# The last weight matrix of a decode kernel: five loads in place of eight, and all its rows summed in one way

## The chip, the cores and the metric

The kernel runs on one core of a Trainium2 chip. TensorE does the matmuls (PE in the profile; PEld is its weight load), VectorE (DVE), ScalarE (ACT) and GpSimd (POOL) the rest, and SyncE (SP) issues nearly all loads. The metric is the device time of one execution in microseconds (us), less is better. Before the change it is 401.04 us, the median of four runs: 400.88, 401.01, 401.08 and 402.25.

## The reference

Two blocks read the same normalised row of 1024 numbers, and their results are added. Block A is attention for one new token over a cache of 65536 keys, with 32 query heads in 4 groups. Block B is a small MLP. All inputs are bfloat16.

```python
q = (x @ wq).reshape(B, Sq, 32, 128)                    # A: x is 1 x 1024
scores = einsum("bhqd,bhkd->bhqk", q, k) * 128 ** -0.5  # k, v: 4 groups, 65536 keys each
o = einsum("bhqk,bhkd->bhqd", softmax(scores), v) @ wo

h  = gelu(layernorm(x) @ w1)                            # B
x1 = x + shifted(h) @ w2                                # S is 1
h2 = gelu(layernorm(x1) @ w3) @ w4                      # w4: 3584 x 1024
return x + A + x1 + h2
```

With one token the shifts of the MLP's mixer leave zeros, so the kernel multiplies w2 by a column of zeros. The change touches only the last product of block B, `h @ w4`, and the store of the result.

## The kernel before, in words

**Loads.** Every large input goes once through SBUF in three buffers of 64 KB a partition (`big`, SLOTS = 3). The class `Stream` holds the order: wq, w3, w1 and w2 together, then K and V of each of eight units, with wo between the last K and the last V, and w4 at the end. `pump` issues the next load on SP's queue (line 172 to 191) when a buffer is free; `done` frees one. A key unit is 32768 keys, 8 MB of K or V. w4 is 7 MB and is issued in the pieces of `W4_PIECES`: 6, 5, 6, 4, 3, 2, 1 and 1 rows (lines 181 to 186). A "row" of w4 here is 1024 numbers on each of 128 partitions, 2 KB a partition; there are FC = 28 of them. Each piece has a semaphore of its own, so TensorE can start on a piece as soon as that piece has landed.

**A key unit.** `compute_k` transposes K on VectorE in four parts (line 359), multiplies by the queries (line 364), takes the maximum and the exponentials (lines 369 to 382) and transposes the probabilities (line 385). `compute_v` multiplies them by V (line 414).

**The result row.** `psB` is one PSUM bank; the first half of the result row stands in partitions 0 to 31 and the second half in partitions 32 to 63, each repeated 32 times, since the left operand is a column broadcast to 32. `row_acc` (line 222) adds one product of 512 columns to one half. Everything that adds to the result goes through it: the input row, the w2 products, the projected rows of groups 0 to 2 (`add_projection`, line 457), the projection of group 3 (`project(3)`, 16 matmuls with `oT`, line 451) and w4 (`compute_w4`, two matmuls of 512 columns a row, line 467). The two halves sit in different column groups of TensorE's array.

**The tail.** The order in which the lines are written is: K of the last unit; the projections of groups 0 to 2 with wo; `add_projection`; V of the last unit with `group_rows` (lines 430 to 444, which end in `oT` of group 3); w4's rows 0 to 10; `project(3)`; w4's rows 11 to 21; and then the part that the change removes. A scheduler of the framework may move an instruction past others on its engine when its inputs are late by its own estimate.

**The last six rows.** Rows 22 to 27 are summed in another way. `quarter_acc` splits the result row into four quarters of 256 columns, in two PSUM banks and four column groups, so that a row costs four matmuls of 256 columns. Rows 22 to 24 (AHEAD = 3) come first. Meanwhile ScalarE copies the sums so far out of `psB` (line 486, `sums`), TensorE adds them to the quarters by fp32 matmuls with single columns of the identity (line 504), and rows 25 to 27 follow. ScalarE copies one half of the quarters to `out_t` (line 509), VectorE the other (line 510), and ScalarE issues the store (line 511). For this the quarters of a half lie 256 columns apart in `out_t`, and the two rows that are stored are partitions 31 and 32.

Of the kernel before, what the change touches and what calls it, by code (L numbers as in the profile page):

```python
# [8 lines left out]
BF16 = mybir.dt.bfloat16  # L9
F32 = mybir.dt.float32  # L10
# [5 lines left out]
P = 128  # L16
# [1 line left out]
SUBS = 4  # L18
SETS = 4
SLOTS = 3  # L20
W4_PIECES = (6, 5, 6, 4, 3, 2, 1, 1)
NARROW = 6
AHEAD = 3


def keep_loaded_weights(nc):
# [68 lines left out]
def kernel(  # L95
# [14 lines left out]
    nc = tc.nc  # L110
# [3 lines left out]
    D = A_x.shape[-1]  # L114
# [7 lines left out]
    FC = F // P  # L122
    UKEYS = P * ROW // DH
    assert DH == P and HQ // HKV == 8 and HKV == 4 and D == 1024 and F == 3584 and S == 1
    assert SK % UKEYS == 0 and sum(W4_PIECES) == FC
    NB = SK // UKEYS
# [8 lines left out]
    ogpool = ctx.enter_context(tc.tile_pool(name="og", bufs=2))  # L135
    ps_S = ctx.enter_context(tc.tile_pool(name="psS", bufs=1, space=bass.MemoryType.PSUM))
    ps_O = ctx.enter_context(tc.tile_pool(name="psO", bufs=1, space=bass.MemoryType.PSUM))
    ps_M = ctx.enter_context(tc.tile_pool(name="psM", bufs=2, space=bass.MemoryType.PSUM))
# [10 lines left out]
    class Stream:  # L149
# [17 lines left out]
        def load(self, it):  # L167
# [13 lines left out]
            elif it == "w4":  # L181
                w4_v = B_w4.rearrange("(m c) n -> m c n", c=FC)
                c0 = 0
                for n in W4_PIECES:
                    go(out=t[:, c0 * D:(c0 + n) * D], in_=w4_v[:, c0:c0 + n, :].rearrange("p c n -> p (c n)"))
# [7 lines left out]
    st = Stream()  # L193
# [6 lines left out]
    ident_f = const.tile([P, P], F32, name="ident_f")  # L200
# [9 lines left out]
    for b in range(2):  # L210
        nc.gpsimd.tensor_copy(
            out=spread[:, 2 * b:2 * b + 2, :].rearrange("p r (a i) -> p r a i", a=4),
            in_=ident_f[:, 64 * b:64 * b + 64].rearrange("p (i r) -> p r i", r=2).unsqueeze(2).to_broadcast([P, 2, 4, 32]))
# [6 lines left out]
    psB = ps_B.tile([P, 512], F32, name="psB")  # L220

    def row_acc(j, lhsT, rhs, start=False):
        nc.tensor.matmul(psB[32 * j:32 * j + 32, :], lhsT=lhsT.to_broadcast([lhsT.shape[0], 32]), rhs=rhs, start=start,  # L223
                         stop=False, tile_position=(0, 32 * j), skip_group_check=True)

    x_t = ppool.tile([P, DC, 32], BF16, name="x_t", tag="p")
    for a in range(4):
        nc.vector.transpose(out=x_t[32 * a:32 * a + 32].rearrange("p c j -> p (c j)"),  # L228
                            in_=x_row[:, 256 * a:256 * (a + 1)].rearrange("p (i c) -> p c i", c=DC))
# [3 lines left out]
    def layernorm(src, tag):  # L233
# [24 lines left out]
    _, xn2_rep, _, _ = layernorm(xn, "b")  # L258
# [14 lines left out]
                          in_=sel8[:].unsqueeze(2).to_broadcast([P, 8, 16]))  # L273
# [43 lines left out]
    hT = const.tile([P, FC], BF16, name="hT")  # L317
# [86 lines left out]
    def compute_v(u):  # L404
        g, b = divmod(u, NB)
        if b == 1:
            og, wb, ol = group_weights()
        vt = st.tiles[("V", u)][:].rearrange("p (s u t d) -> p s u t d", u=SUBS, s=SETS, t=16)
        oacc = ps_O.tile([P, 512], F32, name="oacc")
        pT = group["p"]  # L410
        for e in range(SUBS):
            for t in range(16):
                q = t % 4
                nc.tensor.matmul(oacc[32 * q:32 * (q + 1), :], lhsT=pT[:, e, 32 * t:32 * (t + 1)],  # L414
                                 rhs=vt[:, :, e, t, :], start=(e == 0 and t < 4),
                                 stop=(e == SUBS - 1 and t >= 12), tile_position=(0, 32 * q))
        st.done(("V", u))
        if b == 0:
            og = ogpool.tile([P, 512], F32, name="og", tag="og")
            nc.scalar.copy(out=og[:], in_=oacc[:])  # L420
            group["og"] = og
            return
        nc.vector.scalar_tensor_tensor(out=og[:], in0=oacc[:], scalar=wb[:, 1:2], in1=og[:],  # L423
                                       op0=ALU.mult, op1=ALU.add)
        group_rows(g, og, ol)
# [20 lines left out]
    def project(g):  # L446
        wt = st.tiles["wo"][:].rearrange("p (g j n) -> p g j n", g=HKV, j=8)
        for j in range(8):
            for h2 in range(2):
                if g == HKV - 1:  # L450
                    row_acc(h2, oT[g][:, j:j + 1], wt[:, g, j, 512 * h2:512 * (h2 + 1)])
                    continue
                nc.tensor.matmul(tail["rows"][0:1, h2, :], lhsT=oT[g][:, j:j + 1],  # L453
                                 rhs=wt[:, g, j, 512 * h2:512 * (h2 + 1)], start=(g == 0 and j == 0),
                                 stop=(g == HKV - 2 and j == 7), tile_position=(0, 0))
# [7 lines left out]
    def compute_w4(lo, hi):  # L463
        wt = st.tiles["w4"]
        for c in range(lo, hi):
            for j in range(2):
                row_acc(j, hT[:, c:c + 1], wt[:, D * c + 512 * j:D * c + 512 * (j + 1)])
# [12 lines left out]
    compute_v(NU - 1)  # L480
    early = sum(W4_PIECES[:2])
    compute_w4(0, early)
    project(HKV - 1)
    compute_w4(early, FC - NARROW)
    sums = ogpool.tile([64, 512], F32, name="sums", tag="og")
    nc.scalar.copy(out=sums[:], in_=psB[0:64, :])
    quarters = [ps_M.tile([P, 512], F32, name="pm_r", tag="pm") for _ in range(2)]

    def quarter_acc(lhsT, rhs, start=False):
        for h in range(2):  # L490
            for j in range(2):
                q = 2 * h + j
                nc.tensor.matmul(quarters[h][32 * q:32 * q + 32, 0:256], lhsT=lhsT(j), rhs=rhs(j, h), start=start, stop=False,
                                 tile_position=(0, 32 * q), skip_group_check=True)

    def narrow_rows(lo, hi, start=False):
        wt = st.tiles["w4"]
        for c in range(lo, hi):
            quarter_acc(lambda j: hT[:, c:c + 1].to_broadcast([P, 32]),
                        lambda j, h: wt[:, D * c + 512 * j + 256 * h:D * c + 512 * j + 256 * (h + 1)],  # L500
                        start=start and c == lo)

    narrow_rows(FC - NARROW, FC - NARROW + AHEAD, start=True)
    quarter_acc(lambda j: ident_f[0:64, 32 * j:32 * j + 1].to_broadcast([64, 32]),
                lambda j, h: sums[:, 256 * h:256 * (h + 1)])
    narrow_rows(FC - NARROW + AHEAD, FC)

    out_t = ogpool.tile([64, 2, 256], BF16, name="out_t", tag="og")
    nc.scalar.copy(out=out_t[:, 0, :], in_=quarters[0][0:64, 0:256])
    nc.vector.tensor_copy(out=out_t[:, 1, :], in_=quarters[1][64:128, 0:256])  # L510
    nc.scalar.dma_start(out=out[0, 0, :].rearrange("(j n) -> j n", j=2),
                        in_=out_t[31:33].rearrange("p h n -> p (h n)"))

# [1 line left out]
_INS = ['A_x', 'A_k_cache', 'A_v_cache', 'A_wq', 'A_wo', 'B_x', 'B_w1', 'B_w2', 'B_w3', 'B_w4']  # L515
# [26 lines left out]
```

## Time and profile before

| what | value |
|---|---|
| median of four runs | 401.04 us |
| the profiled execution | 401.08 us |
| its span, first to last instruction | 399.1 us |
| TensorE busy | 236.4 us (59%) |
| VectorE busy | 209.3 us (52%) |
| ScalarE busy | 27.6 us (7%) |
| bytes read | 169.87 MB, 426 GB/s over the span |
| mean granted TensorE clock | 0.795 |

The span leaves out what lies before the first and after the last instruction of the program, 2.0 us in the profiled execution. "Busy" counts an engine's own work, without waits and without issuing loads. The granted clock is the share of TensorE's full clock that a throttle lets through; it is listed for the whole span here and for stretches further on. A group of instructions is named by its line, its engine, and its tiles as out<-in; an "x16" behind it is their number.

### The profile page before, as it was taken

How to read it: one execution, taken by the hardware profiler on the slowest of the kernel's cores; microseconds unless marked ns; L12 is line 12 of the kernel's file. 1: busy time of each engine (PE TensorE's matmuls, PEld its weight loads, DVE VectorE, ACT ScalarE, POOL GpSimd, SP SyncE). 2: the span in 40 equal slices, each digit the busy share in tenths (PEclk: the TensorE clock that was granted, in tenths of full speed). 3: DMA queues.
4: the chain of work that ended last, by engine and by line, in shares of the span. 5: the costliest groups of instructions: out<-in, count | busy, mean ns of one | idle time of the engine just before them, and what ended most of it. 6: DMA issues, size and time to landing. Idle time of an engine off the chain costs nothing.

```text
span 399.1 us, 2590 instructions
## 1 busy us (share of the span) xinstructions
PE 236.4 (59%) x1368; PEld 45.9 (11%) x874; DVE 209.3 (52%) x155; ACT 27.6 (7%) x36; POOL 5.4 (1%) x28
## 2 busy tenths in 40 slices
PE   0561980591569238733974296439462955494987
PEld 0210010010100010011001110101020102010133
DVE  1620010974296559633953795269439942884131
ACT  1001010003000200020002000200100011002000
POOL 2000000000000000000000000000000000000000
PEclk9996886596869787966695689569956896698789
DMA  9998999999999999999999999999999999999996
GB/s 421 420 443 382 438 460 466 434 420 420 415 428 427 453 460 429 420 427 420 427 435 453 453 427 415 427 420 434 440 435 460 427 420 396 427 453 440 392 424 252
DMA packets 4576, 170.03 MB, mean 426 GB/s; under 512 B 467, under 2 KB 469, under 8 KB 982
## 3 DMA queue, kind: packets, MB, share of 16 engines
q1 hardware_dynamic: 4560, 169.87, 98.9%
q8 instruction: 9, 0.15, 0.2%
q14 instruction: 1, 0.01, 0.0%
q10 hardware_dynamic: 6, 0.00, 0.0%
HBM read 169.87 MB, written 0.00 MB: 426 GB/s over the span
## 4 chain that ended last, share of the span: by engine, by line
DMA 53%; PE 24%; DVE 19%; ACT 2%; issue 1%; DVEq 0%; ACTq 0%
DMA big<-in_A_k_cache_dram 44%; DVE big L359 14%; DMA big<-in_B_w_dram 10%; PE sc L364 7%; PE oacc L414 5%; PE o_acc L453 3%; PE psh L289 3%; PE psB L223 3%; DVE mx L369 2%; ACT p_sb L382 2%; DVE p_sb L385 2%; PE ps L336 1%; DVE o_rows L459 0%; DVE m L373 0%; PE pm_mx L371 0%
## 5 line engine op out<-in xcount | busy, mean ns | idle before, releaser
L364 PE MATMUL sc<-big,qdiag 128*128 128x512 bf16 x512 | 130.3, 416 | 61.9 <-DVE big L359 56.5
L359 DVE STREAM_TRANSPOSE big<-big 128x4096 f32<-128x4096 f32 x32 | 139.4, 4413 | 49.5 <-DMA big<-in_A_k_cache_dram 49.5
L414 PE MATMUL oacc<-big,p_sb 128*32 128x512 bf16 x512 | 45.5, 526 | 34.5 <-DVE p_sb L385 34.5
L369 DVE TENSOR_REDUCE mx<-sc 128x1 f32<-128x2048 f32 x8 | 18.3, 2292 | 30.2 <-PE sc L364 30.2
L364 PEld LDWEIGHTS <-qdiag 128*128 128x128 bf16 x128 | 13.2, 103 | 174.6 <-issue 144.6
L382 ACT ACTIVATE p_sb<-sc,nball 128x2048 bf16<-128x2048 f32 x8 | 15.7, 1967 | 218.9 <-DVE nball L380 218.8
L385 DVE STREAM_TRANSPOSE p_sb<-p_sb 128x2048 bf16<-128x2048 bf16 x8 | 18.5, 2311 | 18.0 <-ACT p_sb L382 18.0
L414 PEld LDWEIGHTS <-p_sb 128*32 128x32 bf16 x512 | 16.8, 127 | 59.9 <-DVE p_sb L385 35.1
L289 PE MATMUL psh<-big,ln_rep_b 128*32 128x512 bf16 (+1 forms) x64 | 12.4, 941 | 8.6 <-DMA big<-in_B_w_dram 8.6
L453 PE MATMUL o_acc<-big,oT 128*1 128x512 bf16 x48 | 13.4, 450 | 2.4 <-ACT p_sb L382 2.4
L371 PE MATMUL pm_mx<-ident_f,mx 128*1 128x128 f32 x8 | 2.2, 272 | 19.1 <-DVE mx L369 19.1
L328 DVE STREAM_TRANSPOSE h_row<-h_row 128x896 bf16<-128x896 bf16 x1 | 1.1, 1112 | 21.8 <-ACT h_row L327 21.8
L423 DVE SCALAR_TENSOR_TENSOR og<-oacc,wb,og 128x512 f32<-128x512 f32 x4 | 3.0, 745 | 16.7 <-PE oacc L414 16.7
L459 DVE COPY o_rows<-o_acc 1x1024 f32<-1x1024 f32 x1 | 1.2, 1211 | 14.1 <-PE oacc L414 14.1
L237 PE MATMUL pm_ln<-ln_rowsum_a,ones_f 128*128 128x1 f32 x2 | 0.6, 346 | 12.5 <-DVE ln_rowsum_a L235 12.5
L435 PE MATMUL pm_e<-ol,sel8big 128*128 128x129 f32 x8 | 2.8, 452 | 7.9 <-DVE ol L434 7.9
L313 POOL COPY qdiag<-qx 32x32 bf16<-32x32 bf16 x16 | 3.3, 204 | 279.3 <-PE sc L364 250.7
L228 DVE STREAM_TRANSPOSE x_t<-x_row 32x256 bf16<-32x256 bf16 x4 | 2.5, 616 | 8.1 <-DMA x_row<-in_A_x_dram 8.0
L223 PE MATMUL psB<-big,hT 128*32 128x512 bf16 x44 | 6.5, 448 | 0.0
L289 PE MATMUL psq<-big,ln_rep_a 128*32 128x512 bf16 x64 | 5.2, 497 | 1.3 <-DMA big<-in_A_wq_dram 1.3
L336 PE MATMUL ps<-big,ln_rep_b 128*32 128x512 bf16 x16 | 5.3, 505 | 1.1 <-ACT h_row L327 1.1
L378 PE MATMUL pm_mx<-ident_f,rep 1*128 1x1 f32 x8 | 1.8, 228 | 5.0 <-DVE rep L375 5.0
(101 smaller groups left out, 74.2 us busy)
## 6 DMA issues: line engine op xcount, KB each, us to landing
big<-in_A_wo_dram SPq DMA_DIRECT2D x1, 8192.0 KB, 35.6
big<-in_B_w_dram SPq DMA_DIRECT2D x1, 7168.0 KB, 38.1
big<-in_B_w_dram SPq DMA_DIRECT2D x2, 2048.0 KB, 46.3
big<-in_B_w_dram SPq DMA_DIRECT2D x2, 1536.0 KB, 27.3
big<-in_B_w_dram SPq DMA_DIRECT2D x1, 1280.0 KB, 24.1
big<-in_B_w_dram SPq DMA_DIRECT2D x1, 1024.0 KB
big<-in_B_w_dram SPq DMA_DIRECT2D x1, 768.0 KB, 30.8
big<-in_B_w_dram SPq DMA_DIRECT2D x1, 512.0 KB, 31.5
```

Source lines behind the costliest of these rows:

```text
L223: nc.tensor.matmul(psB[32 * j:32 * j + 32, :], lhsT=lhsT.to_broadcast([lhsT.shape[0], 32]), rhs=rhs, start=start, stop=False, tile_positio ...
L289: nc.tensor.matmul(acc[32 * q:32 * q + 32, i, 0:n], lhsT=rep[:, c, :], rhs=cols(c, i, q), start=(c == 0), stop=(c == DC - 1), tile_positio ...
L313: nc.gpsimd.tensor_copy(out=qdiag[at, LEAD:].rearrange("p (x c) -> p x c", x=4)[:, :, 32 * a:32 * a + 8], in_=qx[at, :, 8 * g:8 * g + 8])
L336: nc.tensor.matmul(ps1[0:32, q, :], lhsT=xn2_rep[:, c, :], rhs=wt[:, 0, c, 512 * q:512 * (q + 1)], start=(c == 0), stop=(c == DC - 1), til ...
L359: nc.vector.transpose(out=words, in_=words)
L364: nc.tensor.matmul(sc[:, e, :], lhsT=qdiag[:, c0:c0 + P], rhs=cols[:, s, e, :, b2, :, r], start=(s == 0 and b2 == 0 and r == 0), stop=(s = ...
L369: nc.vector.reduce_max(out=mx[:], in_=sc[:].rearrange("p e n -> p (e n)"), axis=AX.X)
L382: nc.scalar.activation(out=p_sb[:], in_=sc[:], func=ACTF.Exp, bias=nball[:, b:b + 1], scale=SCALE, accum_out=group["lall"][:, b:b + 1])
L385: nc.vector.transpose(out=flat, in_=flat)
L414: nc.tensor.matmul(oacc[32 * q:32 * (q + 1), :], lhsT=pT[:, e, 32 * t:32 * (t + 1)], rhs=vt[:, :, e, t, :], start=(e == 0 and t < 4), stop ...
L423: nc.vector.scalar_tensor_tensor(out=og[:], in0=oacc[:], scalar=wb[:, 1:2], in1=og[:], op0=ALU.mult, op1=ALU.add)
L453: nc.tensor.matmul(tail["rows"][0:1, h2, :], lhsT=oT[g][:, j:j + 1], rhs=wt[:, g, j, 512 * h2:512 * (h2 + 1)], start=(g == 0 and j == 0), ...
```

## The change

The last six rows are summed like the others, `compute_w4` runs over all 28 rows, and the helper functions of the quarters are removed, with the fp32 matmuls and the copy `sums`. The result is read from `psB` by one copy on ScalarE, 64 partitions by 512 columns, and partitions 31 and 32 are stored. w4 is loaded in five pieces of 11, 9, 5, 2 and 1 rows. The first two of them are still the ones that are written ahead of `project(3)`, so `early` is now 20 rows instead of 11.

```diff
-W4_PIECES = (6, 5, 6, 4, 3, 2, 1, 1)
-NARROW = 6
-AHEAD = 3
+W4_PIECES = (11, 9, 5, 2, 1)
...
     early = sum(W4_PIECES[:2])
     compute_w4(0, early)
     project(HKV - 1)
-    compute_w4(early, FC - NARROW)
-    sums = ogpool.tile([64, 512], F32, name="sums", tag="og")
-    nc.scalar.copy(out=sums[:], in_=psB[0:64, :])
-    quarters = [ps_M.tile([P, 512], F32, name="pm_r", tag="pm") for _ in range(2)]
-
-    def quarter_acc(lhsT, rhs, start=False):
-        for h in range(2):
-            for j in range(2):
-                q = 2 * h + j
-                nc.tensor.matmul(quarters[h][32 * q:32 * q + 32, 0:256], lhsT=lhsT(j), rhs=rhs(j, h), start=start, stop=False,
-                                 tile_position=(0, 32 * q), skip_group_check=True)
-
-    def narrow_rows(lo, hi, start=False):
-        wt = st.tiles["w4"]
-        for c in range(lo, hi):
-            quarter_acc(lambda j: hT[:, c:c + 1].to_broadcast([P, 32]),
-                        lambda j, h: wt[:, D * c + 512 * j + 256 * h:D * c + 512 * j + 256 * (h + 1)],
-                        start=start and c == lo)
-
-    narrow_rows(FC - NARROW, FC - NARROW + AHEAD, start=True)
-    quarter_acc(lambda j: ident_f[0:64, 32 * j:32 * j + 1].to_broadcast([64, 32]),
-                lambda j, h: sums[:, 256 * h:256 * (h + 1)])
-    narrow_rows(FC - NARROW + AHEAD, FC)
-
-    out_t = ogpool.tile([64, 2, 256], BF16, name="out_t", tag="og")
-    nc.scalar.copy(out=out_t[:, 0, :], in_=quarters[0][0:64, 0:256])
-    nc.vector.tensor_copy(out=out_t[:, 1, :], in_=quarters[1][64:128, 0:256])
+    compute_w4(early, FC)
+
+    out_t = ogpool.tile([64, 512], BF16, name="out_t", tag="og")
+    nc.scalar.copy(out=out_t[:], in_=psB[0:64, :])
     nc.scalar.dma_start(out=out[0, 0, :].rearrange("(j n) -> j n", j=2),
-                        in_=out_t[31:33].rearrange("p h n -> p (h n)"))
+                        in_=out_t[31:33, :])
```

## The prediction

> **What bounds the kernel now.** I read the page's slices and DMA queues first, then the landings of the last load, w4, issue by issue, then the instructions of the last 13 us in order of time, then the granted clock in stretches. The page first:
>
> ```profile
> DMA  9998999999999999999999999999999999999996
> GB/s 421 420 443 382 438 460 466 434 420 420 415 428 427 453 460 429 420 427 420 427 435 453 453 427 415 427 420 434 440 435 460 427 420 396 427 453 440 392 424 252
> ...
> q1 hardware_dynamic: 4560, 169.87, 98.9%
> ```
>
> The one queue of loads fills 98.9% of the span at 426 GB/s. Nothing between the first and the last load can save time unless it lets the loads run sooner; only the last slice has room. So the sum is that of the tail: when w4 lands, and what follows a landing. The w4 issues, a row for each (KB, then us from issue to landing):
>
> ```profile
> big<-in_B_w_dram SPq DMA_DIRECT2D x1, 1280.0 KB, 24.1
> big<-in_B_w_dram SPq DMA_DIRECT2D x1, 1536.0 KB, 27.3
> ...
> big<-in_B_w_dram SPq DMA_DIRECT2D x1, 768.0 KB, 30.8
> big<-in_B_w_dram SPq DMA_DIRECT2D x1, 512.0 KB, 31.5
> big<-in_B_w_dram SPq DMA_DIRECT2D x1, 256.0 KB, 31.7
> ...
> big<-in_B_w_dram SPq DMA_DIRECT2D x1, 256.0 KB, 17.4
> ```
>
> SP's timeline has these issues at 362.07, 362.54, 363.49, 363.96, 364.43 and 379.39, so they landed at 386.2 (rows 6 to 10), 389.8 (11 to 16), 394.3 (21 to 23), 395.5 (24, 25), 396.1 (26) and 396.8 (27). The first and fourth issues (rows 0 to 5 and 17 to 20) show no landing. The eighth was issued late because SP waited 14.5 us for the load of V; V therefore landed at 379.4, and w4 takes 396.8 - 379.4 = 17.4 us, or 0.62 us a row.
>
> Then what TensorE does with it (start, us, engine, line):
>
> ```profile
> 386.67 2.04 PE L223 MATMUL psB<-big,hT 128*32 128x512 bf16 x10
> 388.65 0.80 PE L435 MATMUL pm_e<-ol,sel8big 128*128 128x129 f32 x2
> 389.37 1.96 PE L223 MATMUL psB<-big,hT 128*32 128x512 bf16 x12
> 391.17 1.89 PE L223 MATMUL psB<-big,oT 128*32 128x512 bf16 x16
> 392.90 2.11 PE L223 MATMUL psB<-big,hT 128*32 128x512 bf16 x18
> ...
> 395.48 0.58 ACT L486 COPY sums<-psB 64x512 f32<-64x512 f32 x1 [27.80 <-PE psB L223]
> ...
> 396.12 0.64 PE L493 MATMUL pm_r<-sums,ident_f 64*32 64x256 f32 x8 [0.28 <-ACT sums L486]
> ...
> 396.68 0.51 PE L493 MATMUL pm_r<-big,hT 128*32 128x256 bf16 x12
> 397.23 0.37 ACT L509 CAST out_t<-pm_r 64x256 bf16<-64x256 f32 x1 [1.16 <-PE pm_r L493]
> 397.27 0.43 DVE L510 CAST out_t<-pm_r 64x256 bf16<-64x256 f32 x1 [6.81 <-PE pm_r L493]
> 397.77 0.27 ACTq L511 DMA_DIRECT2D out_dram<-out_t  x1
> ```
>
> See two things. First, from 386.67 to 395.5 TensorE has no idle stretch: rows 0 to 10, then the projection of the last group (the 16 with oT), then rows 11 onward. It is behind the loads: rows 11 to 16 landed at 389.8 and began at 392.90. Two matmuls in different column groups run together, so a row of two costs (392.90 - 391.17) / 8 = 0.216 us at full clock. Second, the end hangs on two things at once: the sums chain lets rows 25 to 27 begin at 396.68, and row 27 lands at 396.8. From that landing to the store's issue it is 397.77 - 396.8 = 0.97 us.
>
> The clock, in stretches (the third figure from the right is the granted clock, then the DMA share and GB/s):
>
> ```profile
> 384.40:385.70 1.30, 0.00 (x1) 0.00 (x1) 1.27 (x2) 0.00 (x0) 0.00 (x0) 1.00 1.06 438
> 385.70:387.00 1.30, 1.30 (x8) 0.35 (x10) 1.26 (x2) 0.00 (x0) 0.00 (x0) 1.00 1.00 425
> 387.00:390.40 3.40, 3.40 (x18) 1.25 (x15) 1.95 (x6) 0.00 (x0) 0.00 (x0) 0.50 0.97 406
> 390.40:392.90 2.50, 2.50 (x26) 1.07 (x22) 0.06 (x1) 0.00 (x0) 0.00 (x0) 1.00 0.99 408
> ```
>
> After 1.3 us with no matmul and one more with only the small fp32 ones of the projection's rows, the clock stood at half for 3.4 us. A row cost 0.42 us there (weight loads of two rows at 389.78 and 390.20).
>
> **The change, part by part.**
>
> *Loads.* Eight issues become five: 0.33 to 0.43 us of SP's time each, all in 361.69 to 364.9 while the queue holds V, and the 14.5 us wait for V before the eighth goes. The queue never ran dry around it, so I cost both at nothing; the cover is the queued V, which lands at 379.4. The bytes stay. Larger descriptors may run better: windows of 380 to 384, with 10 and 12 KB descriptors, moved 424 GB/s, and 393 to 394, with 2 to 6 KB ones, 393, at a full DMA share both. A row is 0.262 MB, so 0.62 against 0.67 us; seven rows travelled in pieces of three or fewer, and three will: four rows save at most 4 x 0.05 = 0.2 us, and at least nothing. I take 0.15, near the measured end. New landings: rows 0 to 10 at 386.1 (the old second landing, one piece less), rows 11 to 19 5.6 later at 391.7, rows 20 to 24 at 394.8, 25 and 26 at 396.0, 27 at 396.65.
>
> *The coarser pieces.* Rows 0 to 10 start at 386.67 as before, because the add of the projected rows is ahead of them; 386.1 is still in time. They end as before, and the next matmul can start at 391.17. But `early` is now 20 rows: the projection of the last group stands behind rows 11 to 19 in the written order, and these land at 391.7. TensorE waits 0.5 us with the projection's 16 queued behind it, whose oT is ready (its last DVE step starts at 390.23 and takes 0.23). In the old order the projection covered that time. From 391.7: nine rows 1.94, projection 8 x 0.216 = 1.73, so 395.4; rows 20 to 24 (landed) 1.08, so 396.45; rows 25 and 26 0.43, so 396.9; row 27 starts there, not at 396.65.
>
> *The tail.* Gone: sums copy 0.58, eight fp32 matmuls (0.64 for all), 24 narrow matmuls, and the DVE copy 0.43. Row 27 is now two matmuls of 512 columns, 0.38 us each and side by side: 397.3. One ACT copy of 64x512 then makes the whole output; the row of the same size is the sums copy, 0.58, and ACT began 0.04 after the last matmul there. The 64x256 copy took 0.37, so the price lies between 0.37 and 2 x 0.37; I take 0.58. So 397.9. The store then needs no other engine; it followed DVE's end by 0.07, and I take 0.05 of 0 to 0.07. Issue at 397.93 against 397.77: +0.16 us. What follows the issue is the same.
>
> *Sum.* The profiled execution took 401.08 (span 399.1 and 2.0 around it), 0.04 over the median of 401.04. 401.08 + 0.16 = 401.24; against the median, 401.2.
>
> [...] The trace's row: the clock fell to half after about 2.3 us without wide matmuls, and stayed there 3.4 us. [...] By the row here, a gap of 2 us can cost half the clock, and the rival below lives.
>
> **The rivals.**
>
> *The new gap halves the clock under the last rows (slower).* Place: before rows 11 to 19. If the gap at 384.4 does not halve the clock in an execution, rows 0 to 10 run at 0.216: 386.67 + 2.4 + 0.8 for L435, done near 389.9, and then TensorE is idle until 391.7, 1.8 us. That resembles the gap that did halve it. Half clock for 3.4 us from there on loses 1.7 us of work, and 5.4 us of work (25 pairs of 0.216) stands between 391.7 and the end with no slack: 401.2 + 1.7 = 402.9. It decides for slower from 2.1 us at half clock upward (1.05 us lost, added to 0.16, reaches 0.3%). In the old order the projection starts as soon as oT is there, so the old gap is only some 0.6 us. Against it: the profiled execution has the half clock early, and then the new gap is 0.5 us.
>
> *The projection goes first after all.* Instructions here are reordered: L435 stands between rows 4 and 5 though written ahead of row 0. If the projection is put ahead of rows 11 to 19, it runs 391.17 to 392.9, rows 11 to 19 end at 394.85, rows 20 to 24 at 395.95, rows 25 and 26 at 396.45; row 27 starts at its landing, 396.7. Then 0.38, 0.04, 0.58, 0.05 give 397.75: 401.0. For it: the same reordering. Against: the other rows keep their written order.
>
> *The loads themselves end sooner.* The DMA share falls to 0.75, 0.50 and 0.05 in the windows of 394, 395 and 396: the engines do not end together. If the new pieces made them, the last landing would come 0.25 + 0.5 + 0.76 = 1.5 us sooner, and the time would be about 399.8. Nothing in the change divides the bytes in another way.
>
> **How the numbers follow.** About 0.3% (1.2 us) is what a measurement can tell here. The forecast has 0.52 and the projection first 0.11: both within 0.3%. The halved clock has 0.32 (its condition holds in some executions, and I have one profile): slower. The loads ending together has 0.05: faster. So 0.05, 0.63, 0.32. The range leaves out the last case: from 400.7 (projection first, with the copy at 0.37 and 0.05 more from the loads) to 402.9.
>
> **What would show it.** Right: five w4 issues in a row after 361.69; landings near 386.1, 391.7, 394.8, 396.0, 396.65; the 16 matmuls with oT after 18 with hT; a wait of TensorE near 391.2; ACT's 64x512 copy of 0.58 and the store near 397.9. Wrong: oT's matmuls before rows 11 to 19; a granted clock of 0.50 anywhere after 391.7; a first landing later than 386.67, which would move everything behind it.

## The result and the profile after

The changed kernel takes 401.28 us (median of 33 executions), the one before 400.93 (54 executions). The ratio of the two over all these executions is 1.0022, with a 95% interval of 1.0015 to 1.0028: slower, by less than the 0.3% that the prediction set as its bound.

The median hides the shape. The 33 times fall into two groups with nothing between them: 18 from 400.89 to 401.32 (middle 401.13) and 15 from 402.53 to 402.92 (middle 402.80). The spans, first to last instruction, divide in the same way: 398.8 to 399.2 us and 400.5 to 400.8. The median is simply the highest but one of the lower group. Of the kernel before, 49 of 54 times are below 401.4. The profiled execution of the changed kernel took 402.8, so its trace shows the upper group.

First the loads. The page of the changed kernel, its queue of loads, then the w4 issues that show a landing (KB, us from issue to landing):

```profile
span 400.7 us, 2544 instructions
...
q1 hardware_dynamic: 4128, 169.87, 98.4%
```

```profile
big<-in_B_w_dram SPq DMA_DIRECT2D x1, 2816.0 KB, 24.0
big<-in_B_w_dram SPq DMA_DIRECT2D x1, 2304.0 KB, 29.2
big<-in_B_w_dram SPq DMA_DIRECT2D x1, 1280.0 KB, 31.8
...
big<-in_B_w_dram SPq DMA_DIRECT2D x1, 256.0 KB, 32.7
```

They were issued at 362.00, 362.38, 362.85 and 363.80, so rows 0 to 10 landed at 386.0, rows 11 to 19 at 391.6, rows 20 to 24 at 394.65, row 27 at 396.5. V was issued at 338.00 and landed 41.3 later, so w4 took 17.2 us against 17.4. The loads end sooner than before, and yet the span is 1.6 us longer. The instructions of the tail, in order of time, show where it went:

```profile
386.07 1.24 PE L221 MATMUL psB<-big,hT 128*32 128x512 bf16 x9
387.42 0.49 PE L433 MATMUL pm_e<-ol,sel8big 128*128 128x129 f32 x2
387.84 1.68 PE L221 MATMUL psB<-big,hT 128*32 128x512 bf16 x13
391.58 3.69 PE L221 MATMUL psB<-big,hT 128*32 128x512 bf16 x18 [2.06 <-DMA big<-in_B_w_dram]
395.04 2.08 PE L221 MATMUL psB<-big,oT 128*32 128x512 bf16 x16
396.93 1.91 PE L221 MATMUL psB<-big,hT 128*32 128x512 bf16 x16
...
398.88 0.58 ACT L485 CAST out_t<-psB 64x512 bf16<-64x512 f32 x1 [30.84 <-PE psB L221]
399.48 0.26 ACTq L486 DMA_DIRECT2D out_dram<-out_t  x1
```

The line numbers are two lower than before. TensorE waited 2.06 us for rows 11 to 19, with the projection (the 16 with oT) queued behind them. The nine rows then took 395.04 - 391.58 = 3.46 us, 0.38 a row, where a row costs 0.216 at full clock. The projection's eight pairs took 1.89, most of that at full clock (8 x 0.216 is 1.73). The granted clock of the same execution, third figure from the right:

```profile
384.40:387.00 2.60, 1.98 (x13) 0.66 (x13) 2.53 (x4) 0.00 (x0) 0.00 (x0) 1.00 1.02 435
387.00:388.50 1.50, 1.39 (x13) 0.61 (x12) 0.92 (x4) 0.00 (x0) 0.00 (x0) 1.00 0.95 406
388.50:391.90 3.40, 1.34 (x13) 0.51 (x11) 0.38 (x2) 0.00 (x0) 0.00 (x0) 1.00 0.98 415
391.90:395.40 3.50, 3.50 (x20) 1.44 (x17) 0.00 (x0) 0.00 (x0) 0.00 (x0) 0.51 0.82 334
395.40:398.90 3.50, 3.44 (x32) 1.59 (x28) 0.00 (x0) 0.03 (x1) 0.00 (x0) 1.00 0.07 26
```

In 388.5 to 391.9 TensorE was busy for 1.34 of 3.40 us; in the next 3.5 us it had half the clock, just when the late rows had arrived. In the execution of the kernel before, the half clock lay at 387.0 to 390.4, and here the clock is full in that place.

### The profile page after: what moved, and what is told of

It reads as the page before. It is cut to its first block, busy times and chain, and to the rows that moved or that the text cites. A ratio compares the mean times of both kernels' runs of the same rounds, so it can differ in the third digit from the quotient of the medians.

```text
span 400.7 us, 2544 instructions
## 1 busy us (share of the span) xinstructions
PE 233.3 (58%) x1348; PEld 45.9 (11%) x854; DVE 209.0 (52%) x154; ACT 27.3 (7%) x35; POOL 5.4 (1%) x28
## 3 DMA queue, kind: packets, MB, share of 16 engines
q1 hardware_dynamic: 4128, 169.87, 98.4%
## 4 chain that ended last, share of the span: by engine, by line
DMA 55%; DVE 21%; PE 19%; ACT 2%; another core or an unknown queue 2%; issue 1%; SPq 0%; DVEq 0%; ACTq 0%
DMA big<-in_A_k_cache_dram 42%; DVE big L357 15%; PE sc L362 11%; DMA big<-in_B_w_dram 7%; DMA big<-in_A_wq_dram 5%; PE oacc L412 4%; DVE p_sb L383 2%; DVE mx L367 2%; ACT p_sb L380 2%; PE psB L221 2%; PE psq L287 2%; PE pm_mx L369 0%; DVE m L371 0%; PE pm_mx L376 0%
## 5 line engine op out<-in xcount | busy, mean ns | idle before, releaser
L451 PE MATMUL o_acc<-big,oT 128*1 128x512 bf16 x48 | 12.3, 422 | 2.4 <-ACT p_sb L380 2.4
L221 PE MATMUL psB<-big,hT 128*32 128x512 bf16 x56 | 8.5, 446 | 2.1 <-DMA big<-in_B_w_dram 2.1
```

## The experiments

Two theories stood after this. The gap: the projection now stands behind row 19, so TensorE runs dry between row 10 and row 11 (for 2.06 us at 402.8), and in some executions this halves its clock under the last rows. The rival: the coarse pieces or the wide tail make the upper group in themselves. The line numbers below are each kernel's own; each verdict compares with the kernel before on the same chip.

**The projection in the gap.** Only its place is changed:

```diff
-    early = sum(W4_PIECES[:2])
+    early = W4_PIECES[0]
```

> The changed kernel, but with the projection of the last group behind the first piece (rows 0 to 10) and not behind the second. Theory (the new gap between row 10 and row 11 halves TensorE's clock under the last rows in some executions): the projection now stands in that gap, so the upper group of times near 402.8 is gone or under one in ten, and the median is 400.9 to 401.05, like the kernel before. Rival (the wide last rows or the coarser pieces make the upper group): the upper group stays at about 15 of 33, and only the lower group moves, from 401.13 to about 400.95.

Eleven executions, 400.63 to 401.22, median 400.85; the kernel before 400.99; ratio 0.9989 (0.9979 to 0.9999). There is no upper group. That the kernel is also faster than the one before is not shown: nine of the 29 executions of the kernel before on this chip took 401.44 to 402.41, with spans of 398.8 to 399.2 like the others, so that their extra time lies before the first or after the last instruction. The ratio leans on them. The two medians are 0.14 us apart, the medians of the spans 0.1 (398.8 and 398.9). The same 29 executions stand behind the ratios of the next three experiments. The tail of this one:

```profile
389.35 1.95 PE L221 MATMUL psB<-big,hT 128*32 128x512 bf16 x13
390.91 2.10 PE L221 MATMUL psB<-big,oT 128*32 128x512 bf16 x16
392.64 4.21 PE L221 MATMUL psB<-big,hT 128*32 128x512 bf16 x34
...
396.88 0.58 ACT L485 CAST out_t<-psB 64x512 bf16<-64x512 f32 x1 [29.23 <-PE psB L221]
397.49 0.26 ACTq L486 DMA_DIRECT2D out_dram<-out_t  x1
```

There is no wait between the three lines of matmuls, and the store is issued at 397.49 instead of 397.77. This profile has its half clock early, at 386.5 to 389.9; that the late one is gone rests on the eleven times. Coarse pieces and wide rows are both still in this kernel, so neither makes the upper group alone, nor do the two together, as long as the projection stands behind row 10.

**Other work in the gap.** The order stays the changed kernel's; four pairs of matmuls that nobody needs go between row 10 and row 11:

```diff
-    compute_w4(0, early)
+    compute_w4(0, W4_PIECES[0])
+    filler(4, lambda i, j: st.tiles["w4"][:, D * i + 512 * j:D * i + 512 * (j + 1)])
+    compute_w4(W4_PIECES[0], early)
     project(HKV - 1)
```

> The changed kernel with four pairs of extra matmuls of rows already landed, into a bank that nobody reads, between row 10 and row 11; order and loads are the changed kernel's. Theory (clock): 0.9 us of the 2.1 us gap is filled, the upper group shrinks to under one in ten, and the median is 401.1 to 401.4 (where the clock halved early, the filler itself delays row 11 by up to 0.4). Rival (the backlog of the projection alone makes the upper group, whatever the clock): the upper group stays near 402.8 at 15 of 33.

Eleven executions, 401.05 to 401.88, median 401.14 (before 400.99; ratio 1.0002, 0.9994 to 1.0011). The upper group is gone although the projection is as late as in the changed kernel. So a late projection with no idle time before it leaves the kernel 0.15 above the one before, and the 1.67 us between the groups needs the idle time. In this kernel's profile, which has its half clock early (386.0 to 389.5) and so would have had a short gap, the filler ran and the next rows followed with no wait; that the filler also serves in a gap of 2 us rests on the eleven times:

```profile
390.64 1.24 PE L471 MATMUL pm_f<-big,hT 128*32 128x512 bf16 x8
391.60 2.22 PE L221 MATMUL psB<-big,hT 128*32 128x512 bf16 x18
393.54 2.01 PE L221 MATMUL psB<-big,oT 128*32 128x512 bf16 x16
```

**The tail alone.** The changed kernel with the old pieces, which puts the projection back behind row 10:

```diff
-W4_PIECES = (11, 9, 5, 2, 1)
+W4_PIECES = (6, 5, 6, 4, 3, 2, 1, 1)
```

> The kernel before with its eight pieces and its projection behind row 10, but all rows wide and one copy at the end: the tail part of the change alone. Theory: one group of times; from the landing of row 27 it is 0.04 + 0.38 + 0.04 + 0.58 + 0.05 = 1.09 us to the store against 0.97 before, so 401.0 to 401.1. Rival (the tail makes the upper group): two groups, 15 of 33 near 402.8.

Twelve executions, 401.00 to 401.32, median 401.12 (before 400.99; ratio 0.9998, 0.9990 to 1.0007). One group, as expected; the medians differ by 0.13, and the interval does not tell that from nothing. In the profile row 27 starts at 396.78, takes 0.39, the copy 0.58, and the store is issued at 397.81, 1.03 us after the row's start.

**The loads alone.** The kernel before with the five pieces and nothing else; `early` becomes 20 rows by itself:

```diff
-W4_PIECES = (6, 5, 6, 4, 3, 2, 1, 1)
+W4_PIECES = (11, 9, 5, 2, 1)
```

> The kernel before with the five pieces (so the projection stands behind row 19), but the narrow last rows and two copies kept: the loads part of the change alone. Theory: the gap is there, so two groups with about 15 of 33 in the upper one, 1.5 to 1.9 above the lower; the lower group at 401.0 to 401.2. Rival (the tail is what costs): one group at 400.8 to 401.0, with the loads' gain of up to 0.2.

Six executions: 401.61, 403.00, 403.20, 403.77, 404.09 and 404.70 (before 400.99; ratio 1.0053, 1.0032 to 1.0074). Two groups, but the upper one reached further than expected, and the lower one was higher. The same kernel was profiled three more times for that:

> The kernel of the fourth experiment once more, one look, for a profile of its upper group, which was 403.0 to 404.7 where 402.5 to 402.9 was expected. Theory: half clock after 391.6 as in the changed kernel, with the copy of the sums and the fp32 additions behind the delayed rows adding to it, 1 us or more. Rival: another cause, such as loads that land later.

> The kernel of the fourth experiment, one more look for a profile of its upper group (403.0 to 404.7); the two profiles so far, at 401.61 and 401.41, had the half clock before 391. If it falls there: half clock behind the gap, and the sums copy and the fp32 additions later by as much as the rows ahead of them; if the loads land later instead, the last landing is over 1 us behind 396.6.

> The same again, for the same question: in the upper group, half clock behind the gap and everything behind row 11 later; in the lower, 401.4 to 401.7 as in the two profiles so far.

They took 401.41, 403.04 and 401.62. The profile of the second is of the upper group:

```profile
391.51 3.81 PE L223 MATMUL psB<-big,hT 128*32 128x512 bf16 x18 [2.22 <-DMA big<-in_B_w_dram]
395.13 1.91 PE L223 MATMUL psB<-big,oT 128*32 128x512 bf16 x16
...
397.51 0.58 ACT L486 COPY sums<-psB 64x512 f32<-64x512 f32 x1 [29.66 <-PE psB L223]
...
398.14 0.64 PE L493 MATMUL pm_r<-sums,ident_f 64*32 64x256 f32 x8 [0.34 <-ACT sums L486]
398.70 0.51 PE L493 MATMUL pm_r<-big,hT 128*32 128x256 bf16 x12
...
399.80 0.27 ACTq L511 DMA_DIRECT2D out_dram<-out_t  x1
```

```profile
388.40:391.70 3.30, 1.08 (x11) 0.31 (x7) 0.25 (x2) 0.00 (x0) 0.00 (x0) 0.99 0.96 405
391.70:395.30 3.60, 3.60 (x20) 1.54 (x18) 0.00 (x0) 0.00 (x0) 0.00 (x0) 0.54 0.85 348
```

A wait of the same kind (2.22 us) and the same half clock behind it. The profile at 401.62 is of the lower group:

```profile
391.66 2.12 PE L223 MATMUL psB<-big,hT 128*32 128x512 bf16 x18 [0.32 <-DMA big<-in_B_w_dram]
...
398.26 0.27 ACTq L511 DMA_DIRECT2D out_dram<-out_t  x1
```

There the copy `sums` starts at 395.97; copy and store are both 1.54 later in the upper group's profile. The narrow tail is the worse partner for late rows, since the copy `sums`, the fp32 additions and rows 25 to 27 stand one behind the other after row 21. From the start of row 11 to the store it needs 8.29 us here and 6.60 in the lower group's profile; the changed kernel, with the wide tail, needs 7.90 and 6.21, so 0.39 less both times. The lower group at 401.4 to 401.6 fits that. The times of 403.2 to 404.7 have no profile, but their spans are 401.0 to 401.5, where that of the execution at 403.04 is 401.0. So at most 0.5 of the up to 1.7 us that they have over it lies between the first and the last instruction; what the rest outside is stays open.

**The earlier gap filled.** The half clock at 387.0 to 390.4 of the kernel before followed an earlier gap, behind V. Six pairs of matmuls of V's rows fill it in the changed kernel:

```diff
+        if u == NU - 1:
+            filler(6)
         st.done(("V", u))
```

> The changed kernel with six pairs of extra matmuls (rows of V, into a bank that nobody reads) behind the last V matmul, in the earlier gap, where TensorE waits 1.3 us for the copy of the projected rows. Theory: the earlier gap then never halves the clock, so nothing but the gap behind row 10 decides: the upper group grows from 15 of 33 to over half, and no profile shows half clock between 386 and 391. Rival (the earlier gap has no part in it): the shares stay as they are. If the upper group vanishes, the theory of the two gaps is wrong.

Twelve executions: six from 400.99 to 401.26 and six from 402.66 to 402.79 (before 400.94; ratio 1.0022, 1.0011 to 1.0034). Six of 12 is no telling number against 15 of 33, so the expected growth was not shown. The profile, of the lower group, shows more. The wait before row 11 is 1.55 us, from 389.99 to 391.54, and the clock is full on both sides of it:

```profile
386.30:389.70 3.40, 3.08 (x27) 1.33 (x26) 2.38 (x6) 0.00 (x0) 0.00 (x0) 1.00 1.02 435
389.70:393.10 3.40, 1.85 (x19) 0.83 (x17) 0.00 (x0) 0.00 (x0) 0.00 (x0) 1.00 0.94 393
393.10:396.50 3.40, 3.40 (x34) 1.77 (x32) 0.00 (x0) 0.00 (x0) 0.00 (x0) 1.00 0.57 228
```

So an execution can fall in the lower group without any half clock in its tail. The early half clock is one way to escape the late one, not the only one. Here the gap was 0.5 us shorter than the one of 2.06.

**A longer gap.** The kernel just shown, with the first piece shortened and the second lengthened, so that the second lands as before but TensorE runs dry sooner:

```diff
-W4_PIECES = (11, 9, 5, 2, 1)
+W4_PIECES = (6, 14, 5, 2, 1)
```

> The kernel of the fifth experiment (early gap filled) with pieces of 6, 14, 5, 2 and 1 rows: the second piece still ends at row 19 and lands as before, but the first has only six rows, so TensorE runs dry near 388.4 and waits about 3 us for row 6 instead of about 1.7 for row 11. [...] Rival (the share of the upper group does not hang on the length of the gap): 6 of 12 again, median near 403 or below with both groups of like size.

Five executions: 402.91, 403.69, 403.69, 403.82 and 404.16 (before 401.02; ratio 1.0064, 1.0050 to 1.0077). Four, from 403.69 to 404.16, have spans of 401.6 and 401.7. The fifth, 402.91, has a span of 400.1, shorter by 1.5: by its span it belongs to the lower group, and 2.8 us lie outside its span, where three of the others have 2.1. By their spans both groups are about 1 us higher than the changed kernel's (400.5 to 400.8 and 398.8 to 399.2); rows 6 to 10 now stand behind the wait, 5 x 0.216 = 1.08 us at full clock. Four of five against six of 12 is too few to show that the share grew. The profile, of an execution at 403.69, has a wait of 2.83 us before row 6:

```profile
389.20:392.60 3.40, 1.21 (x12) 0.67 (x13) 0.00 (x0) 0.00 (x0) 0.00 (x0) 1.00 0.93 390
392.60:396.00 3.40, 3.40 (x20) 1.44 (x16) 0.00 (x0) 0.00 (x0) 0.00 (x0) 0.50 0.70 282
```

**The narrow tail on the better order.** The kernel before with the five pieces and with `early = W4_PIECES[0]`:

> The kernel before with the five pieces and the projection behind the first of them: the narrow tail on the order of the first experiment. Theory: one group; the last landing is 0.15 to 0.2 sooner, and the narrow tail is 0.1 shorter than the wide one where the sums chain is done in time: 400.7 to 400.85. Rival (the narrow tail hangs on the sums chain and not on the landing): 400.9, no better than the wide tail of the first experiment at 400.85.

Eleven executions, 400.70 to 401.35, median 400.90 (before 400.94; ratio 0.9997, 0.9988 to 1.0005): the rival's number, no better than the wide tail at 400.85. The copy `sums` starts at 395.19, and the fp32 additions hold row 25 until 396.39, so its tail hangs on that chain. The lowest median of the study is the first experiment's.

**The changed kernel once more**, for a profile of its lower group:

> The changed kernel once more, one look, for a profile of its lower group. If it falls there (18 of 33 did): half clock ends before 392, rows 11 to 19 start near 391.6, the store is issued near 397.9, and the time is 401.1 to 401.3. If it falls in the upper group: half clock after 391.6 again, 402.5 to 402.9.

It took 401.66, 0.34 over the highest of the lower group. The loads are late as a whole: row 11 starts at 392.12, not 391.58. From there on it is the lower group's course:

```profile
386.74 2.32 PE L221 MATMUL psB<-big,hT 128*32 128x512 bf16 x9
...
389.71 1.77 PE L221 MATMUL psB<-big,hT 128*32 128x512 bf16 x13
392.12 2.12 PE L221 MATMUL psB<-big,hT 128*32 128x512 bf16 x18 [0.63 <-DMA big<-in_B_w_dram]
394.06 1.91 PE L221 MATMUL psB<-big,oT 128*32 128x512 bf16 x16
395.78 1.91 PE L221 MATMUL psB<-big,hT 128*32 128x512 bf16 x16
```

Its half clock lies at 386.5 to 389.9, the rows 0 to 10 are slow, and the wait is 0.63 us. From row 11 to the store's issue (398.33) it is 6.21 us; in the upper group's profile it is 399.48 - 391.58 = 7.90. The difference, 1.69, is the distance between the groups.

## Why the prediction was right, and where it was not

**The time** was right: 401.2 forecast, 401.28 measured, inside the range, within 0.3%. But that was luck in good part. The median sits at the edge of two groups; had two of the 18 fallen in the upper group, it would have been 402.5, which is the slower rival's side. The forecast describes the lower group, whose middle is 401.13, and whose one profile has its course: a wait of 0.63 us where 0.5 was forecast, no half clock behind it. The kernel before, too, came out 0.11 lower over 54 executions than in the four ahead of the forecast, so that the medians are 0.35 us apart where 0.16 was forecast.

**Landings.** 386.1, 391.7, 394.8 and 396.65 were forecast; 386.0, 391.6, 394.65 and 396.5 came. The loads' gain was put at 0.15 us of at most 0.2, and the profiles, one of each kernel, have 17.4 - 17.2 = 0.2. That larger descriptors are the reason was not tested.

**The order** was right: the projection stands behind row 19, and the rival of the projection going first did not occur. Made by hand, it gave 400.85 where that rival's price was 401.0.

**The step that failed** is "They end as before, and the next matmul can start at 391.17". It took one execution's half clock for a fixed part of the kernel. Where that half clock is not there, rows 0 to 10 end at 389.5, the gap is 2.06 us instead of the forecast 0.5, and at 402.8 half clock followed it. (The rival's own 1.8 us for this gap took the 0.80 of L435 from the half clock; at full clock it is 0.49.) The prediction had this as its slower rival, with a price of 1.7 us against the 1.67 measured, a time of 402.9 against 402.80, and a chance of 0.32; 15 of 33 executions took it. What it described (half clock for 3.4 us behind the gap, here from 391.95 to 395.36) and its price were right; that a median of such a mixture falls in one group or the other was not said.

**The tail.** From the last matmul's end (1.91 after 396.93, 398.84) the copy began 0.04 later, took 0.58, and the store followed its end by 0.02: all as forecast, except 0.02 for 0.05.

**The loads ending together** did not occur: the last landing came at 396.5, where that rival needed one near 395.3.

**Where the granted clock changes.** What the prediction read from its own row, that a gap of 2 us can cost half the clock, came back: waits of 2.06, 2.22 and 2.83 us were followed by half clock, in one profile each. The trace of the kernel before has 39 changes of the granted clock and that of the changed kernel 37, between 1.00 and 0.50, each a whole multiple of 3.41 us after the one before it (3.41 to 20.48 us). They fall at other places in the program from one execution to the next. So the tail can be laid out in steps of 3.41 us, counted from a change. The first two lines are steps of the changed kernel's profile at 402.8, the last two of its profile at 401.66:

```profile
381.71:385.12 3.41, 2.08 (x31) 0.84 (x26) 1.43 (x2) 0.00 (x0) 0.00 (x0) 1.00 0.97 406
385.12:388.54 3.42, 3.25 (x23) 1.18 (x21) 2.77 (x6) 0.00 (x0) 0.00 (x0) 1.00 1.01 431
...
383.10:386.51 3.41, 2.08 (x19) 0.54 (x14) 2.07 (x3) 0.00 (x0) 0.00 (x0) 1.00 1.00 420
386.51:389.92 3.41, 3.41 (x15) 1.21 (x15) 1.63 (x3) 0.00 (x0) 0.00 (x0) 0.50 0.97 413
```

Both executions have the earlier gap, the one behind V: 1.33 us without a matmul, then 1.05 us (at 402.8) and 1.13 us (at 401.66) of the four fp32 matmuls that add the projected rows, each of a single row (one partition). At 402.8 the edge of a step at 385.12 divides the fp32 matmuls from nearly all that precedes them, and the two steps hold 1.91 and 2.36 us of other matmuls. The clock stays full, rows 0 to 10 are done at 389.52, and the gap behind row 10 is 2.06 us. At 401.66 the gap and most of the fp32 matmuls lie in one step, which holds 1.25 us of other matmuls, and the next step has half the clock; the gap behind row 10 is 0.63 us. The four profiles of the loads alone agree: in the three lower ones (401.61, 401.41 and 401.62) rows 0 to 10 are slow for a part (their weight loads come every 0.43 us, where a row at full clock costs 0.216) and done at 391.01, 390.93 and 391.34, and the waits behind them are 0.64, 0.62 and 0.32 us; at 403.04 they are done at 389.28, and the wait is 2.22 us. So in these six profiles an early half clock goes with the lower group. That its place among the steps of 3.41 us decides the group is the author's reading; no experiment set the place.

How busy TensorE was ahead of half clock can be read for some stretches. Ahead of the late one it was busy for 1.35 of 3.41 us (388.54 to 391.95, the changed kernel at 402.8), 1.08 of 3.30 (the loads alone at 403.04) and 1.21 of 3.40 (the longer gap); the 1.85 of 3.40 us around the wait of 1.55 us were followed by full clock. Ahead of the early half clock it was busy for 2.08 of 3.41 us, in the kernel before (383.58 to 386.99) and in the changed kernel at 401.66, and the step at 402.8 with the same 2.08 us was followed by full clock. So busy time alone does not tell these cases apart. Without the fp32 matmuls of a single row the three steps hold 1.11, 1.25 and 1.91 us. Whether those matmuls are the reason was not tested, and no run shows a limit.

## What to carry to other kernels

When loads bound a kernel, as they do this one (98.4% of the span), the order of the ready work can still matter (median 400.85 with the projection first, 401.28 without): put work whose inputs are already there (here a projection) ahead of work that waits for a load, so that the wait is filled. What an idle stretch of TensorE costs can show only behind it: here waits of 2.06, 2.22 and 2.83 us were followed by half clock for 3.4 us, just when the late data had arrived and no slack was left; one of 1.55 us was not, and that execution took 401.08. Look at the list of all times, not only at the median: two groups with nothing between them ask for a profile of each, and the span beside each time tells what lies outside the program's instructions.

## What had not been expected of the hardware

- Matmuls that nobody needs made the kernel more even: with 0.9 us of them in the gap, 11 of 11 executions were below 401.9, against 18 of 33 without.
- One and the same kernel has its half clock in different places from one execution to the next: at 386.5 to 389.9 in one profile of the changed kernel and at 391.9 to 395.4 in another, with the same instructions in the same order.
